# A fused RWKV-6 attention and token mixer: stores moved to the SP queue, and the engines' orders taken from one explicit table of steps

## The chip, the core and the metric

One of the eight cores of a Trainium2 chip runs the whole program. The time is device microseconds from start to end of one execution. The kernel before takes 123.53 us (median of 4 runs beside the new kernel, 122.84 to 123.75). The profile is one traced execution; its span (122.0 us before) is a little shorter than the device time.

Engines in the profile: PE is TensorE's matmuls, PEld its weight loads, DVE is VectorE, ACT is ScalarE, POOL is GpSimd, SP is the engine that here only issues DMAs. A name with q (ACTq, SPq) is that engine's sequencer.

## The reference

Batch 4, 8 heads, 768 tokens, head size 48. A linear attention with a decaying state, then a mixer over tokens:

```python
# attention, per batch and head, t = 0..767
y[t]  = r[t] @ (state + (u * k[t]) ⊗ v[t])
state = w[t][:, None] * state + k[t] ⊗ v[t]
# mixer, x = y as [batch, 768, 384]
W   = (x @ w_q) @ (x @ w_k).T / sqrt(64)      # no softmax, so it is associative
out = relu(W @ x) @ w_out
```

The kernel works in chunks of 128 tokens, two chunks to a unit: 12 units of 256 tokens, 3 units to a batch. With logs of w summed over a chunk by matmuls, r and k are scaled by decays, and the attention of a chunk becomes ordinary masked products, plus a product with the state.

## The kernel before

Each unit n goes through some thirty steps. Those that matter here, with the engine of each (cut; `T` holds the tiles by name):

```python
def load(n, nm, ap):   # SP: 384 KB; three buffers for each of w, k, r, v
    t = ld.tile([C, H, D2], F32, name=nm + "G", tag=nm + "G")
    nc.sync.dma_start(out=t, in_=src.rearrange("h (p j) d -> p h (j d)", j=2))
def log(n):    nc.scalar.activation(pad(T["lw", n]), jhd(T["w", n]), ACT.Ln, ...)    # ACT, reads w
def sums(n):   ...   # PE: cw = prefix sums of the logs
def expk(n), expr(n), decay(n): ...  # ACT: exp(-cw), exp(cw), the chunk's decay
def kdec(n):   nc.gpsimd.tensor_tensor(pad(T["Kd", n]), jhd(T["k", n]), ...)         # POOL, reads k
def rdec(n):   nc.vector.tensor_tensor(pad(Rd)[:, j], jhd(T["r", n])[:, j], ...)     # DVE, reads r
def vcast(n):  nc.scalar.copy(V2, jhd(T["v", n]))                                    # ACT, reads v
def uk1(n), uk2(n): ...  # POOL: k*u, then times r;   red(n): DVE sums it;  vd(n): POOL, times v
def trR(n, j), evT(n): ...   # PE transposes Rd and Kd into PSUM; DVE copies them out (RKT)
def amat(n, js), mask(n, js): ...    # PE scores, DVE mask multiply
def state(n), stadd(n, q), stev(n, q): ...     # PE, PE, DVE: the state after each chunk
def ymat(n), yst(n), yd(n), yev(n): ...        # PE: Y from scores, state, diagonal; copied out as X
def xtr(n), xev(n), qkmat(n), qkev(n): ...     # X transposed, its q and k
# per batch b: tmat, tev, mix, mixev, fin, finev, store
def yst(n):
    for q in range(2):
        if 2 * m + q:
            for hp in range(NP):
                mm(T["Y", n][:, q, ds(hp * D2, D2)], T["RKT", n][:, 0, q, hp],
                   SB[:, ds(hp * D2, D2)], start=False)
```

The order of an engine's instructions is that of a plan: each step has an offset from the start of its unit, the units start some 7.6 us apart, and the plan is sorted by time. All inner units share one list of offsets (`steps`), the first and the last have their own. Tuples of 0 and 1 (`EX`, `ET`, `EQ`, `EM`, `EF`) choose for each PSUM copy between VectorE and ScalarE; `ES` does so for the issuing queue of each half store.

```python
steps = [(-3.67, log, ()), (-1.33, uk1, ()), (-0.45, sums, ()), (-0.42, expk, ()), ...   # cut
start = [0.42, 8.84, 16.14, 23.73, 31.34, 38.86, 46.52, 54.11, 61.53, 69.25, 76.58, 84.42]
```

## Time and profile before

| What | kernel before |
|---|---|
| device time, median | 123.53 us |
| span of the profiled execution | 122.0 us |
| first prefix sum on TensorE | 7.08 us |
| TensorE busy from there to its last matmul | 98.6 us |
| TensorE idle from there to its last matmul | 9.9 us |
| after the last matmul | 6.4 us |

The last four rows add up to the span; they are taken with the end of the last matmul at 115.58 us. (The prediction cuts at 115.2 us and so has 98.2 and 6.8 for the second and the last.) Only idle time of TensorE, its start and the tail can be won, since the matmuls stay.

### The profile page before, as it was taken

The numbers are of one execution on the slowest core, as the hardware profiler recorded it, in microseconds if no ns is written. First come the engines' busy times: TensorE is split into PE (matmuls) and PEld (weight loads), VectorE is DVE, ScalarE is ACT, GpSimd is POOL, SyncE is SP. The second block draws the span as 40 slices with busy tenths as digits, with TensorE's granted clock in tenths as the row PEclk, the third lists the DMA queues.
The fourth block names the chain that finished last, engine by engine and source line by source line (L and its number), as shares of the span: only waits on it lengthen the run. The fifth ranks groups of instructions, "written<-read, shape, count | busy, mean of one in ns | idle before, by whom it ended". The sixth has DMA issues, their size and how long they took to land.

```text
span 122.0 us, 4284 instructions
## 1 busy us (share of the span) xinstructions
PE 100.1 (82%) x1822; PEld 64.6 (53%) x1822; DVE 91.8 (75%) x150; ACT 77.2 (63%) x146; POOL 84.7 (69%) x81
## 2 busy tenths in 40 slices
PE   0193938979898999999999899999999999966800
PEld 0133536557575766757657466576576666532400
DVE  6213596699798978999989998989989777253800
ACT  4236391689779868986685948976478966426000
POOL 8949899995999999599597995967839804000000
PEclk9999996799999999999999999999999999999985
DMA  3999999999999999899839999500552200573092
GB/s 77 322 325 325 323 320 341 292 232 318 236 256 273 288 300 263 230 266 247 245 75 329 348 269 252 149 0 0 134 129 52 82 5 0 129 181 85 24 283 83
DMA packets 54598, 24.66 MB, mean 202 GB/s; under 512 B 51121, under 2 KB 54578, under 8 KB 54578
## 3 DMA queue, kind: packets, MB, share of 16 engines
q1 hardware_dynamic: 52274, 21.24, 64.6%
q10 hardware_dynamic: 2304, 3.15, 9.1%
q8 instruction: 14, 0.23, 0.7%
q14 instruction: 6, 0.05, 0.1%
HBM read 19.66 MB, written 4.72 MB: 200 GB/s over the span
## 4 chain that ended last, share of the span: by engine, by line
PE 68%; ACT 12%; DVE 6%; DMA 3%; POOL 3%; issue 2%; ACTq 1%; SPq 1%; DVEq 0%
PE cw L66 12%; PE Y L66 11%; PE psT L66 10%; PE fps L66 10%; PE Sn L66 5%; PE A L66 5%; PE xt_ps L66 5%; PE qk L66 5%; PE Tps L66 4%; ACT X L130 3%; DMA u<-in_u_dram 3%; DVE AmB L244 3%; ACT XT L130 2%; PE mps L66 2%; POOL uk L250 1%
## 5 line engine op out<-in xcount | busy, mean ns | idle before, releaser
L244 DVE TENSOR_TENSOR AmB<-A,MASK 128x1024 bf16<-128x1024 f32 x24 | 28.8, 1219 | 1.3 <-PE A L66 1.2
L271 POOL TENSOR_TENSOR Vd<-V,diag 128x768 bf16<-128x768 bf16 x12 | 17.7, 1478 | 13.7 <-ACT X L130 3.4
L250 POOL TENSOR_TENSOR uk<-kG,ubc 128x768 f32<-128x768 f32 x12 | 21.8, 1816 | 1.7 <-DVE ubc L486 1.7
L178 ACT ACTIVATE em<-cw,bias 128x384 bf16<-128x384 f32 x24 | 13.0, 580 | 15.6 <-PE cw L66 15.6
L257 POOL TENSOR_TENSOR uk<-uk,rG 128x768 f32<-128x768 f32 x12 | 21.8, 1816 | 0.1
L207 POOL TENSOR_TENSOR KdS<-kG,em 128x768 bf16<-128x768 f32 x12 | 19.7, 1640 | 1.2 <-ACT em L178 1.2
L227 DVE COPY RKT<-psT 128x2048 bf16<-128x2048 bf16 x12 | 14.6, 1217 | 4.0 <-PE psT L66 4.0
L66 PEld LDWEIGHTS <-KdS 64*128 64x128 bf16 (+1 forms) x256 | 10.8, 99 | 9.1 <-POOL KdS L207 3.6
L200 DVE TENSOR_TENSOR RdS<-rG,cw 128x384 bf16<-128x384 f32 x24 | 12.2, 551 | 4.5 <-ACT cw L185 4.5
L66 PE MATMUL fps<-wout_sb,mixT 128*128 128x384 bf16 x72 | 14.6, 328 | 0.1
L302 DVE TENSOR_TENSOR SB<-Sn,pt 128x384 bf16<-128x384 f32 x20 | 11.0, 551 | 4.0 <-PE Sn L66 2.6
L66 PEld LDWEIGHTS <-RKT 48*64 48x64 bf16 (+1 forms) x464 | 10.3, 107 | 7.1 <-issue 4.5
L185 ACT ACTIVATE cw<-cw,bias 128x384 f32<-128x384 f32 x24 | 12.3, 553 | 0.2
L264 DVE TENSOR_REDUCE diag<-uk 128x16 f32<-128x768 f32 x12 | 11.3, 945 | 0.4 <-POOL uk L257 0.4
L155 ACT ACTIVATE logw<-wG 128x768 bf16<-128x768 f32 x12 | 10.2, 851 | 2.1 <-DMA wG<-in_w_dram 2.1
L66 PE MATMUL cw<-logw,BI 128*128 128x384 bf16 x36 | 11.5, 377 | 0.0
L66 PE MATMUL psT<-ID,KdS 128*128 128x128 bf16 x96 | 7.8, 227 | 4.0 <-DVE AmB L244 2.0
L66 PE MATMUL cw<-logw,BS 128*128 128x384 bf16 x36 | 11.0, 363 | 0.0
L66 PE MATMUL A<-RKT 48*64 48x128 bf16 x384 | 10.1, 226 | 0.8 <-ACT X L130 0.8
L130 ACT CAST X<-Y 128x768 bf16<-128x768 f32 x11 | 8.8, 800 | 2.9 <-PE Y L66 2.7
L211 ACT CAST V<-vG 128x768 bf16<-128x768 f32 x12 | 10.0, 841 | 0.0
L130 ACT COPY osb<-fps 128x384 f32<-128x384 f32 x13 | 6.1, 484 | 5.3 <-PE fps L66 2.1
(74 smaller groups left out, 165.1 us busy)
## 6 DMA issues: line engine op xcount, KB each, us to landing
wG<-in_w_dram SPq DMA_DIRECT2D x12, 384.0 KB, 5.5
kG<-in_k_dram SPq DMA_DIRECT2D x12, 384.0 KB, 5.1
rG<-in_r_dram SPq DMA_DIRECT2D x12, 384.0 KB, 4.8
vG<-in_v_dram SPq DMA_DIRECT2D x12, 384.0 KB, 4.9
out_dram<-osb ACTq DMA_DIRECT2D x16, 192.0 KB, 3.0
out_dram<-osb SPq DMA_DIRECT2D x8, 192.0 KB, 3.8
wout_f<-in_moe_w_out_dram SPq DMA_DIRECT2D x1, 576.0 KB, 4.7
wq_f<-in_moe_w_q_dram SPq DMA_DIRECT2D x1, 96.0 KB, 4.1
```

The costliest lines, as they stand in the source:

```text
L66: nc.tensor.matmul(o, l, rr, start=start, stop=stop, skip_group_check=True, is_transpose=trans)
L130: (nc.scalar.copy if e else nc.vector.tensor_copy)(o, i)
L178: nc.scalar.activation(em[:, j], T["cw", n, 1 + j][:, 0:DM], ACT.Exp, bias=bias[2 + j], scale=-1.0)
L185: nc.scalar.activation(cw, cw, ACT.Exp, bias=bias[j], scale=1.0)
L200: nc.vector.tensor_tensor(pad(Rd)[:, j], jhd(T["r", n])[:, j], T["cw", n, j][:, 0:DM].rearrange("p (h d) -> p h d", d=D), ALU.mult)
L207: nc.gpsimd.tensor_tensor(pad(T["Kd", n]), jhd(T["k", n]), hd(T["em", n]), ALU.mult)
L227: nc.vector.tensor_copy(RKT, T["psT", n])
L244: nc.vector.tensor_tensor(T["AmB", n][:, js].rearrange("p q h t -> p h q t"), T["A", n, js], _rep(_rep(MASK[:, js], 1, NP), 1, 2), ALU.mult)
L250: nc.gpsimd.tensor_tensor(uk, T["k", n].rearrange("p h (j d) -> p h j d", j=2), _rep(ubc.rearrange("p (h d) -> p h d", d=D), 2, 2), ALU.mult)
L257: nc.gpsimd.tensor_tensor(uk, uk, T["r", n].rearrange("p h (j d) -> p h j d", j=2), ALU.mult)
L264: nc.vector.tensor_reduce(diag.rearrange("p j h -> p h j"), T["uk", n], axis=AX.X, op=ALU.add)
L271: nc.gpsimd.tensor_tensor(Vd, T["V2", n], _rep(T["diag", n], 3, D), ALU.mult)
```

## The change

The intent: free ScalarE's queue of store issues, balance ScalarE and VectorE anew, and replace the offsets by one explicit order of all 540 steps, laid out by a list schedule, so that a step of any unit can go where there is room for it. The set of steps is the same in both kernels. The diff, cut to its core:

```diff
-    EX = (1, 1, 1, 1, 1, 1, 1, 1, 1, 1, 1, 0)      ...
-    ES = (1, 0, 0, 1, 0, 1, 1, 1, 1, 1, 1, 0, 1, 1, 1, 1, 1, 1, 0, 1, 0, 1, 0, 0)
+    EX = (0, 1, 1, 1, 0, 1, 1, 1, 1, 1, 1, 1)      ...   # EQ and nearly all EF now 1: ScalarE
+    ES = (0, 0, 0, 0, 0, 0, 0, 0, 0, 0, 0, 0, 0, 0, 0, 0, 0, 0, 0, 1, 0, 1, 0, 1)
-    sm = ctx.enter_context(tc.tile_pool(name="sm", bufs=3))
+    sm = ctx.enter_context(tc.tile_pool(name="sm", bufs=5))
     # trR, amat, XT: the two token halves j as an outer dimension of the tiles (cut)
                 for hp in range(NP):
-                    mm(T["Y", n][:, q, ds(hp * D2, D2)], T["RKT", n][:, 0, q, hp],
-                       SB[:, ds(hp * D2, D2)], start=False)
+                    for j in range(2):
+                        mm(T["Y", n][ds(j * HC, HC), q, ds(hp * D2, D2)],
+                           T["RT", n][:, j, hp, ds(q * HC, HC)], SB[:, ds(hp * D2, D2)],
+                           start=False)
-    steps = [(-3.67, log, ()), ...]            # and first, last, bsteps, blast, start, ... (cut)
+    order = (
+        (load, 0, "w"), (load, 0, "k"), (uload,), (load, 0, "r"), (load, 0, "v"),
+        (load, 1, "w"), (load, 1, "k"), (load, 1, "r"), (log, 0), (load, 1, "v"),
+        (load, 2, "w"), (load, 2, "k"), (sums, 0), (load, 2, "r"), (load, 2, "v"),
+        (load, 3, "w"), (expk, 0), (wload,), (decay, 0), (kdec, 0), (ucast,), (expr, 0),
+        ...
+        (stev, 1, 0), (trR, 2, 0), (red, 2), (trR, 2, 1), (log, 4), (stadd, 1, 1), (decay, 3),
+        (vd, 1), (stev, 1, 1), (load, 7, "w"), (log, 5), (evT, 2), (ymat, 1), (vcast, 3),
+        (load, 8, "w"), (yst, 1), (vd, 2), (rdec, 3), (yd, 1), (vcast, 4), (load, 6, "v"),
+        ...
+    )
     with tc.manual_schedule():
-        for _, _, fn in sorted(plan, key=lambda x: x[:2]):
-            fn()
+        for fn, *a in order:
+            fn(*a)
```

(Options for transposes by DMA were added too; they are all off.)

## The prediction

> **What bounds the kernel now.** I read four views in this order: busy shares of the page, busy time in stretches, the early matmuls in the timeline, then the groups by shape and the issue rows of the stores. The page first:
>
> ```profile
> PE 100.1 (82%) x1822; PEld 64.6 (53%) x1822; DVE 91.8 (75%) x150; ACT 77.2 (63%) x146; POOL 84.7 (69%) x81
> PE   0193938979898999999999899999999999966800
> ```
>
> TensorE is busy 82% of 122.0 us, and its row of slices shows where the rest is: at both ends and in holes of the first third. The stretches give the size (columns: from:to, length, then busy us of PE, PEld, DVE, ACT, POOL, then granted clock, DMA share, GB/s):
>
> ```profile
> 8.00:24.00 16.00, 11.58 (x163) 7.75 (x163) 9.28 (x12) 9.46 (x18) 15.39 (x10) 0.89 1.15 323
> 24.00:40.00 16.00, 13.87 (x311) 9.76 (x313) 14.63 (x20) 13.23 (x25) 14.52 (x10) 1.00 1.00 261
> 40.00:60.00 20.00, 19.75 (x384) 13.34 (x383) 18.70 (x28) 15.94 (x30) 17.12 (x11) 1.00 0.99 260
> 60.00:80.00 20.00, 19.18 (x405) 12.50 (x403) 18.72 (x27) 15.57 (x31) 17.78 (x12) 1.00 0.83 233
> 80.00:100.00 20.00, 19.93 (x393) 13.26 (x392) 17.54 (x26) 13.93 (x29) 12.99 (x8) 1.00 0.24 61
> 107.00:115.20 8.20, 5.99 (x54) 3.15 (x54) 4.51 (x10) 2.98 (x7) 0.00 (x0) 1.00 0.37 95
> ```
>
> From 40 to 100 us TensorE idles 60 - 58.86 = 1.1 us: no order can win there. It idles 4.4 us in 8 to 24, 2.1 in 24 to 40, and 2.2 in 107 to 115.2, in all 9.9 us between the first useful matmul at 7.1 us and the last. So 122.0 = 7.1 of start + 98.2 of matmuls + 9.9 of idle + 6.8 after the last matmul (last copy, last stores).
>
> ```profile
> 5.53 1.62 PE L66 MATMUL ups<-u,one 1*128 1x384 f32 x2 [5.53 <-DMA u<-in_u_dram]
> 7.08 0.50 PE L66 MATMUL cw<-logw,BI 128*128 128x384 bf16 x1
> 11.29 1.03 PE L66 MATMUL psT<-ID,KdS 128*128 128x128 bf16 x8 [1.87 <-POOL KdS L207]
> 18.17 0.61 PE L66 MATMUL psT<-ID,KdS 128*128 128x128 bf16 x8 [2.02 <-DVE AmB L244]
> 20.05 1.04 PE L66 MATMUL psT<-ID,RdS 128*128 128x128 bf16 x8
> ```
>
> The start: the broadcast of u stands first on TensorE and holds the prefix sums back until 7.08, though the logarithm they read ended at 4.98. The same eight transposes take 1.03, 0.61 and 1.04 us: until about 16 us and again in 19 to 22.4 us the array runs at half speed. (The granted clock reads 1.00 before its first record, so there the durations decide.)
>
> The rows that price the changed part, each with busy us and mean ns, then the issue row of the stores (shortest, median, longest ns):
>
> ```profile
> L66 PE MATMUL Y<-SB,RKT 128*128 128x96 bf16 x80 | 5.5, 208 | 0.0
> L66 PEld LDWEIGHTS <-RKT 128*128 128x128 bf16 x80 | 3.8, 98 | 0.5
> L66 PEld LDWEIGHTS <-qks 128*64 128x64 bf16 x48 | 2.3, 109 | 1.2 <-DVE qks L130 0.2
> L66 PE MATMUL qk<-XT,wq_sb 128*64 128x128 bf16 x72 | 4.3, 227 | 0.0
> L434 ACTq DMA_DIRECT2D out_dram<-osb x16: 602/626/754, 57.6 to 115.3; - x16
> ```
>
> **What the Trainium skill says.** "TensorE: Matmul & The Clock Gate", Part 1 (the HAM clock gate): the array runs at half clock until one window of about 3.4 us was busy, and falls back after an idle one. The trace agrees: the hole of 2.0 us ending at 18.17 is followed by 3.4 us of slow matmuls. "TensorEngine Tiling (Array Packing)", Restrictions: column tiling turns Fast Weight Load off. The trace agrees weakly: a load of 64 columns takes 109 ns, one of 128 columns 98. "DMA: Bandwidth & Descriptors", Issuing engines are not separate DMA queues: issuing from a second engine saves only the sequencer's time, usually small. Here it is not small: 626 ns of ScalarE's queue each.
>
> **The change part by part.**
> Stores: 16 of 24 issues stand on ScalarE now, 3 afterwards. That frees 13 x 0.626 = 8.1 us of ScalarE's queue and puts as much on SP, which waits mostly.
>
> Copies: ScalarE takes over 6 casts of qks (0.377), 9 copies of osb (0.484), 2 of XT (0.80) and 2 of mixT (0.50), and gives up one of X (0.80): +2.3 + 4.4 + 1.6 + 1.0 - 0.8 = +8.5 us. VectorE loses 6 x 0.42 + 9 x 0.55 + 2 x 0.55 + 2 x 0.55 - 0.96 = 8.7 us. ScalarE's queue comes out even (77.2 + 16 x 0.63 = 87 before, 85.7 + 3 x 0.63 = 88 after), VectorE falls from 92 to 83. Neither is the bound in 40 to 100 us, so this pays only in holes: I count -0.7 us, about a quarter of the 3.2 us idle in 24 to 100, no more, because the new table also has tight spots (the scores of unit 7 are needed 0.65 us of TensorE work after the second score product, while the mask multiply alone takes 1.22).
>
> Layout: transposes, scores, XT and their copies keep count and sizes. Only the product of state and R changes: 4 matmuls of 128x128 weights per chunk become 8 of 128x64, in 20 chunks, so 80 more. Before, 8 of them take 0.45 us from their start to the next group's (52.59 to 53.04): 56 ns each. For 8 of 128x64 with 96 columns the nearest kin is qk from wq_sb, 128x64 and 128 columns alternating between the halves, six in 0.29 us: 48 ns. If the halves overlapped fully, 28 ns (the 64x96 state products); if they follow kin, 48. I take 41: 20 x (8 x 0.041 - 4 x 0.056) = +2.1 us, between 0 and +3.2. With TensorE full this lands on the end.
>
> Start: the prefix sums now come before u, so they start at 5.0 instead of 7.1, and POOL's first K product precedes its u product, about 2.2 us earlier. The u matmul hides in the wait for it. But the early stretch is also bound elsewhere: up to the Y product of unit 1 the table gives VectorE 18.4 us (17.4 before) and ScalarE 20.5 (19.7), by row durations. From an arrival 2.1 us earlier I keep 1.2. A denser start should warm the array one window sooner: matmuls lose some 4.6 us to the half clock now (half of about 6.2 us busy before 15.6 and 3.1 in 19 to 22.4), and I take 0.8 off. Together -2.0 us.
>
> End: before, the X transpose, its copy and qk of the last unit leave TensorE idle 0.46 + 0.65 = 1.1 us; the new table puts output products of batch 2 between them: -1.1 us. The last six copies go from VectorE (2.97 us in one run) to ScalarE, 6 x 0.484 with two issues of 0.63 between: 4.15, so +1.2; the very last pair of stores goes out on two queues, not one after the other: -0.6. Together +0.5 us with rounding against me.
>
> Buffers: five instead of three for the state remove a wait that the trace does not show; 0. Loads on SP keep their lead; 0.
>
> Sum: -0.7 + 2.1 - 2.0 - 1.1 + 0.5 = -1.2 us, 122.1 us against 123.3.
>
> **The rivals.**
> A, the order wins outright: the halves overlap fully (0 instead of +2.1) and the array stays warm from about 9 us (another -1.5). For it: the Tps products, 128x64 too, run twelve of 384 columns in 1.06 us, 88 ns each, where one alone needs some 165. It would make 118.5 to 120.
> B, TensorE's added matmuls win: +3.2, and the early stretch stays VectorE's, so the start keeps 0.5. For it: the kin at 48 ns, and a table that no longer repeats one pattern per unit, units coming in pairs (by rows, ScalarE has 10.0 us of work against TensorE's 5.4 between the Y products of units 0 and 1). Result 124 to 125.
> C, the tail turns into ScalarE's: after the Y product of unit 11 begins, ScalarE has 13.0 us of work against TensorE's 10.9. Against it: most can start at once, and the mix copies are still split 4 to 2. If true, +1 more.
> D, stores and loads on one queue: a store waiting on SP holds a load back. Against it: the last loads stand just after the first stores, 30 us ahead of their use. 0.
>
> **Range and chances.** The terms in doubt are the halves (-2.1 to +1.1 around mine), the early stretch (-2 to +1.5), the middle and tail (-0.5 to +1.5). Together about 2.3 us either way for 8 in 10, a little wider for unmodelled order effects: 119.2 to 125.0. Faster by over 2% means below 120.9, which needs A or luck in two terms: 0.33. Slower means above 125.8: 0.09. Within 2%: 0.58.
>
> **What would show it.** Right: the first prefix sum at 5.0 us; state-times-R row x160 with a stretch of 0.6 to 0.7 us for 16 of them; TensorE busy 1 to 3 us more; VectorE near 83, ScalarE near 86; holes before the last transposes gone; last matmul to end near 7.3 us. Wrong: the 16 products in 0.45 us or less (rival A); holes over 3 us in all between 40 and 100 us, or a first third as long as before (rival B); TensorE waiting on ScalarE's copies after 105 us (C); compute waiting on a load (D). A span below 119 with TensorE no less busy would mean that I underrated the idle that an order can remove.

## The result, and the profile after

The new kernel takes **127.35 us** (126.94 to 128.50, 4 runs) against 123.53 us beside it: ratio 1.0334, 95% interval 1.0254 to 1.0414. A ratio here is the mean time of the one kernel's fast runs over that of the other's in the same rounds, so it is not quite the ratio of the medians. It is slower by 3%, and the predicted range (119.2 to 125.0) missed it. All ratios below are to the kernel before in the same series.

The page of the new kernel, busy shares and TensorE's row of slices:

```profile
PE 99.7 (79%) x1902; PEld 65.3 (52%) x1902; DVE 84.3 (67%) x132; ACT 85.3 (68%) x164; POOL 84.6 (67%) x81
PE   0399688674598877989999997999899999995700
```

VectorE and ScalarE came out as predicted (83 and 86). TensorE has no more work than before, yet there are holes in slices 5 to 16 of 40, some 12.5 to 50 us. In stretches (same columns as in the prediction):

```profile
8.00:24.00 16.00, 12.84 (x216) 8.22 (x216) 12.70 (x17) 11.38 (x22) 15.43 (x10) 1.00 1.12 311
24.00:40.00 16.00, 11.57 (x243) 7.93 (x241) 9.68 (x13) 10.73 (x20) 11.92 (x8) 0.89 1.02 269
40.00:60.00 20.00, 16.98 (x360) 11.32 (x361) 16.73 (x24) 16.10 (x30) 17.38 (x12) 1.00 1.03 274
80.00:100.00 20.00, 19.31 (x407) 13.43 (x407) 18.02 (x22) 13.78 (x30) 16.95 (x11) 1.00 0.27 67
```

Between 24 and 60 us TensorE idles 4.4 + 3.0 = 7.4 us, where it idled 2.1 + 0.25 before. From 24 to 40 us all the other engines are less busy than before too; from 40 to 60 us ScalarE and POOL are about as busy as before. None of them is full, so none is the bound. The granted clock of 0.89 in the second row is one stretch of 3.4 us at half clock (34.1 to 37.5 us); in the 3.4 us before it TensorE idled 1.8 us. The sum by which we compare:

| | before | after | difference |
|---|---|---|---|
| first prefix sum | 7.1 | 5.1 | -2.0 |
| TensorE busy, to its last matmul | 98.6 | 99.7 | +1.1 (the u product, 1.6 us, now lies inside) |
| TensorE idle, to its last matmul | 9.9 | 13.5 | +3.6 |
| after the last matmul | 6.4 | 7.2 | +0.8 |
| span | 122.0 | 125.5 | +3.5 |

The pages also give the chain of work that ended last, followed back from the end, as shares of the span by engine. Before, then after:

```profile
PE 68%; ACT 12%; DVE 6%; DMA 3%; POOL 3%; issue 2%; ACTq 1%; SPq 1%; DVEq 0%
PE 53%; DMA 21%; ACT 9%; issue 4%; POOL 3%; DVE 3%; SPq 2%; ACTq 1%
```

DMA's share of the chain grew from 3% to 21%. The new kernel's chain runs from 23.8 to 43.0 us through three loads and the two ScalarE steps that read them, the V cast and a log (start, length, what; two short pieces lie between):

```profile
23.81 5.86 DMA wG<-in_w_dram
29.70 5.96 DMA vG<-in_v_dram
35.73 0.83 ACT V L211
37.05 5.09 DMA wG<-in_w_dram
42.16 0.84 ACT logw L155
```

Who waits for the loads? The view of waits lists engine and line, what ended the wait, the total us, how many times, and the longest. Of the new kernel:

```profile
ACT logw L155 <- DMA wG<-in_w_dram: 7.3, 6, 2.3
POOL uk L265 <- DMA kG<-in_k_dram: 6.3, 5, 2.6
DVE RdS L200 <- DMA rG<-in_r_dram: 1.3, 2, 1.1
ACT V L211 <- DMA vG<-in_v_dram: 0.4, 1, 0.4
```

Of the kernel before, the one such line of an input (its first load):

```profile
ACT logw L155 <- DMA wG<-in_w_dram: 2.1, 1, 2.1
```

Three engines now wait for inputs, some 15 us in all, of which about 2.2 us is the first load, as before. The traces also tell for each load when it was issued and landed, and when the first instruction that reads it began. For k and w, in us:

| unit | k before: landed, used | k after: landed, used | w before: landed, used | w after: landed, used |
|---|---|---|---|---|
| 3 | 22.6, 26.7 | 26.2, 26.2 | 21.5, 28.1 | 18.8, 18.8 |
| 4 | 28.4, 34.8 | 33.4, 33.5 | 27.1, 34.3 | not told, 26.4 |
| 6 | 34.7, 48.0 | 49.5, 49.7 | 33.5, 48.9 | 34.4, 34.5 |
| 7 | 46.1, 56.1 | 51.4, 51.6 | 45.0, 56.2 | 40.6, 40.7 |
| 9 | 67.6, 71.5 | 62.3, 64.6 | 66.3, 69.7 | 47.1, 47.1 |

Before, an input of these units lies ready 3 to 15 us ahead of its use (unit 5, not shown, had the least: 0.9 us for k, 1.4 for w). After, most are used as they land. The new table asks for the w of unit 9 at 47 us, before the k of units 6 and 7. The queue shows the same from the other side. SP's issues in the new kernel's timeline (start, length, queue):

```profile
17.94 2.25 SPq L150 DMA_DIRECT2D wG<-in_w_dram  x1
20.28 2.32 SPq L150 DMA_DIRECT2D kG<-in_k_dram  x1
22.71 1.01 SPq L150 DMA_DIRECT2D rG<-in_r_dram  x1
23.81 1.10 SPq L150 DMA_DIRECT2D wG<-in_w_dram  x1
25.00 2.17 SPq L150 DMA_DIRECT2D vG<-in_v_dram  x1
27.27 1.17 SPq L150 DMA_DIRECT2D kG<-in_k_dram  x1
```

Each issue keeps SP 1.0 to 2.3 us, one after the other. The page's GB/s row stands at 321 to 335 up to some 22 us, and at 235 to 308 from there to 50 us. At 322 GB/s 384 KB take 1.22 us, at the lower rates 1.3 to 1.7 us. So SP's order is the order of arrival, and about one input arrives per 1.2 to 1.7 us. The k of unit 4, issued at 27.27, stands behind the w of unit 5 and the v of unit 4. POOL pays for it, with the idle time before in brackets:

```profile
26.23 1.81 POOL L265 TENSOR_TENSOR uk<-kG,ubc 128x768 f32<-128x768 f32 x1 [1.26 <-DMA kG<-in_k_dram]
33.51 1.81 POOL L265 TENSOR_TENSOR uk<-kG,ubc 128x768 f32<-128x768 f32 x1 [2.60 <-DMA kG<-in_k_dram]
```

One more comparison, for the product of state and R, in which I expected most of the new cost. The kernel before, then the new one (timelines of TensorE; the group's time is from its start to the next group's):

```profile
52.59 0.51 PE L66 MATMUL Y<-SB,RKT 128*128 128x96 bf16 x8
53.04 0.50 PE L66 MATMUL Y<-Vd,PERM 64*128 64x384 bf16 x4
```

```profile
55.31 0.53 PE L70 MATMUL Y<-SB,RKT 128*64 128x96 bf16 x16
55.77 0.62 PE L70 MATMUL psT<-ID,RdS 128*128 128x128 bf16 x8
```

Sixteen matmuls of 128x64 take 0.46 us, eight of 128x128 took 0.45. This part costs nothing; by these durations the two halves overlap.

### The profile page after: what moved, and what is told of

The parts are those of the page before. It is cut to its first block, busy times and chain, and to the rows that moved or that the text cites. A ratio compares the mean times of both kernels' runs of the same rounds, so it can differ in the third digit from the quotient of the medians.

```text
span 125.5 us, 4453 instructions
## 1 busy us (share of the span) xinstructions
PE 99.7 (79%) x1902; PEld 65.3 (52%) x1902; DVE 84.3 (67%) x132; ACT 85.3 (68%) x164; POOL 84.6 (67%) x81
## 4 chain that ended last, share of the span: by engine, by line
PE 53%; DMA 21%; ACT 9%; issue 4%; POOL 3%; DVE 3%; SPq 2%; ACTq 1%
DMA wG<-in_w_dram 11%; PE Y L70 9%; PE cw L70 9%; PE fps L70 8%; PE psT L70 7%; DMA vG<-in_v_dram 5%; DMA wout_f<-in_moe_w_out_dram 5%; PE Sn L70 4%; PE qk L70 4%; PE A L70 4%; PE Tps L70 3%; PE xt_ps L70 3%; PE mps L70 3%; POOL KdS L207 2%; DVE AmB L259 2%
## 5 line engine op out<-in xcount | busy, mean ns | idle before, releaser
L70 PE MATMUL fps<-wout_sb,mixT 128*128 128x384 bf16 x72 | 13.9, 327 | 0.3 <-DVE mixT L437 0.3
L134 ACT COPY osb<-fps 128x384 f32<-128x384 f32 x22 | 10.0, 482 | 5.5 <-PE fps L70 4.3
L435 ACT ACTIVATE mixT<-mps 128x384 bf16<-128x384 f32 x20 | 8.9, 493 | 2.9 <-PE mps L70 2.8
L134 ACT CAST X<-Y 128x768 bf16<-128x768 f32 x10 | 8.0, 799 | 3.5 <-PE Y L70 3.5
```

The source lines that it names most:

```text
L70: nc.tensor.matmul(o, l, rr, start=start, stop=stop, skip_group_check=True, is_transpose=trans)
L134: (nc.scalar.copy if e else nc.vector.tensor_copy)(o, i)
```

## The theories and the experiments

Theory L: the loads. The table uses inputs earlier and in another order than one queue can bring them, and engines that run strictly in order wait at their head while TensorE runs dry. It has two parts that can be told apart: the order of the loads on SP, and the place in the table of the steps that read them. Theory O, the rival: the table's order of compute steps stalls TensorE by itself (steps too close behind their producers, units bunched in pairs), and the waits on loads only coincide. Side questions: the layout, the stores, the choice of engines, the start, the end.

### 1. Both kernels without loads after unit 2

```diff
 def load(n, nm):
+    if n >= 3:
+        T[nm, n] = T[nm, n - 3]      # compute on the data of units 0 to 2
+        return
```

The result is wrong; all compute steps and their order stay.

> The new kernel with no input loads after unit 2 (units 3 to 11 compute on the data of units 0 to 2; the result is wrong on purpose). Theory L (inputs arrive too late for the new table, TensorE idles behind engines that wait for them): the extra idle of 24 to 60 us goes, 118 to 121.5 us, well below the 123.5 of the kernel before. Theory O (the new table stalls TensorE by its own order of compute steps, loads only coincide): within 1.5 us of the new kernel, 126 to 128 us.

> The kernel before with no input loads after unit 2 (result wrong on purpose). Its trace has no compute wait on a load after the first, so both theories say 122.5 to 123.6 us, unchanged. If it falls by over 1 us, the loads cost the old order something that the waits do not show, such as contention.

Measured: new table 121.67 us (ratio 0.9877, interval 0.9818 to 0.9936), old order 122.41 us (0.9917, 0.9881 to 0.9954). The loads cost the new table 127.35 - 121.67 = 5.7 us and the old order 123.53 - 122.41 = 1.1 us, a little over the 1 us at which I had said that they cost something which the waits don't show. The difference, 4.6 us, less the 0.7 us by which the new table is better without loads, is the 3.8 us of the result. TensorE in the new kernel without loads:

```profile
24.00:40.00 16.00, 14.20 (x345) 10.28 (x345) 13.74 (x18) 14.05 (x25) 16.00 (x11) 1.00 0.02 4
40.00:60.00 20.00, 18.66 (x401) 12.56 (x399) 17.64 (x25) 16.88 (x34) 18.80 (x12) 1.00 0.05 11
```

It idles 1.8 + 1.3 us there instead of 7.4, and the stretch at half clock is gone. Theory O is out as the cause of the loss. What the whole change gains apart from the loads is small: 0.7 us.

### 2. The layout alone

The old order, engines, stores and state buffers in the new kernel's tiles.

> The kernel before (order of steps, engines, stores, three state buffers) with only the new layout: transposes, XT, and the state-times-R product as 160 matmuls of 128x64. In the new trace sixteen of them take 0.46 us, as eight took before, so 123.0 to 124.0 us, no difference. If my predicted cost of 2.1 us were right after all: 125.5.

Measured: 123.55 us, ratio 1.0003 (0.9970 to 1.0037). The layout is free.

### 3. The loads in order of use

```diff
+    # each load goes out in the order in which the table first reads its data,
+    # as soon as the last reader of its buffer has passed (cut)
+    order = by_first_use(order)
```

Compute steps untouched. A second kernel has five buffers per input besides.

> The new kernel with its loads put in the order in which the table first uses them, compute steps untouched. Theory L1 (the order of the loads is at fault: w and v of later units go ahead of k and r of nearer ones): 121 to 124 us. Theory L2 (the table asks for data ahead of the rate at which the queues deliver it, in whatever order): 125 to 127 us, the waits move from k to w. Theory O: 127 us, unchanged.

> The new table with loads in order of use and five buffers per input instead of three, so that almost no load waits for a buffer. Theory L2a (the rate of the queues is the limit): waits on w remain and it stays over 124.5 us. Theory L2b (loads were issued too late because their buffers were still held): 121.5 to 123.5 us.

Measured: the first 124.28, 127.08, 127.29 and 129.07 us, with a granted clock of 0.985 in the fastest and 0.976 in the slowest run. Only the fastest counts as fast, and the three others, the profiled one among them, are slow by the rule for runs (over 1.5% above the fastest). So what the order of loads is worth alone stays undecided. With five buffers 124.93 and 125.93 in the fast runs (ratio 1.0138, 1.0035 to 1.0241), others to 127.9. That is better than the new kernel's 1.0334, but no cure. In the profiled, slow run of the first, the waits on w still come to 6.3 us, those on k to 5.5 and on v to 4.9. So order and buffers together don't cure a table that asks too early, and theory L2 of the expectation, the rate, is left for what remains. By the count of the table, 35 of the 48 loads are read before TensorE has done 32.2 us of its work (steps priced by the rows of the kernel before); in the old order, before 50.5 us. At 1.22 us each, after 4.1 us for the first and with 2.4 us for the weights, the 35th can't land before some 48 us (an estimate from these traces' numbers, and a lower bound, since the rate falls after 22 us). In the traces the 35th load landed at 53.9 us in both kernels: the queue is no slower than before, the table only asks earlier.

### 4. The readers moved later

Three kinds of steps read inputs well ahead of need: the logs (w), the V casts (v) and the first u product (k). They are moved later, to a fixed amount of TensorE work ahead of their own readers, about where the old order had them. TensorE's and VectorE's orders stay as they are.

```diff
+    for what, reader, lead in ((log, sums, 300), (vcast, state, 400), (uk1, uk2, 250)):
+        order = later(order, what, reader, lead)     # lead in 10 ns of TensorE work, units 3 to 11
+    order = by_first_use(order)
```

> The new kernel, correct, with the logs, the V casts and the first u product of units 3 to 11 moved later, to 3.0, 4.0 and 2.5 us of TensorE work ahead of their readers (where the old order had them), and loads in the order of use. TensorE's and VectorE's orders are untouched. Theory L2 (ScalarE and POOL, strict in order, wait at their head for inputs that the table asks for ahead of the rate of the queues): the waits on w and k nearly vanish, 121 to 123.5 us, close to the 121.7 without loads. Rival H (the early logs are what keeps TensorE fed; or SP and the buffers are at fault): 125 us or more.

> The same kernel as late_by_use, whose profile fell into an execution of 445 us on a disturbed chip. Theory L2 as there: fast runs 123 to 125 us (the two of before had 124.2 and 125.6), waits of ScalarE and POOL on w and k under 3 us in all (13.6 in the new kernel).

Measured: of four runs of the first, one took 446.69 us with TensorE busy 97% of the span, a disturbed chip (a run of the kernel before in the same series took 212.4); the fast ones took 125.58 and 124.20 (ratio 1.0094, 0.9979 to 1.0209), the fourth 128.62, a slow one. Repeated, 123.85 us (123.58 to 124.01), ratio 0.9986 (0.9949 to 1.0024). Nearly all of the loss is gone, and of the waits on inputs only the first remains, 2.3 us. Yet it lacks 2.2 us to the run without loads. The stretches show where:

```profile
80.00:100.00 20.00, 16.75 (x361) 11.28 (x360) 15.58 (x20) 12.50 (x25) 15.31 (x10) 1.00 0.17 42
```

TensorE idles 3.2 us in 80 to 100 us; the new kernel idled 0.7 there. In that window VectorE's sum waits 3.1 us for POOL's second u product, two times, and its copy of the transposes, for which TensorE waits, stands behind that sum. So I had moved the u products of the last units too late, with nothing to gain: their k lies ready by then.

### 5. Which of the readers, and does the order of loads matter beside them?

```diff
-    ((log, sums, 300), (vcast, state, 400), (uk1, uk2, 250))
+    late_uk_to_7:     u products only for units 3 to 7
+    late_no_uk:       u products not moved at all
+    late_logs:        logs alone
+    late_by_release:  as late_uk_to_7, but each load where its buffer comes free (as the new table has it)
+    late_by_use_5:    all three, five buffers per input
```

> As late_again, but the u products move later only for units 3 to 7; for 8 to 11, whose k has landed with slack, they stay where the table has them. If the late u products made the 3.3 us of idle TensorE in 80 to 100 us (0.7 in the new kernel): 121 to 122.5 us. If something else: 123.5 to 124.

> Logs and V casts late, u products all where the table has them, loads in order of use. If only ScalarE's early logs were at fault: like late_uk_to_7. If POOL waiting at its head for k is a cause of its own: 1 to 2.5 us slower, with waits of POOL on k of 3 us or more.

> Only the logs late, V casts and u products where the table has them, loads in order of use. If the logs, whose w the queue must bring first, are the whole cause on ScalarE: 122 to 123 us, like late_no_uk. If the early V casts hold ScalarE too: 123.5 to 125.5 us, with waits of V on its load.

> The steps of late_uk_to_7 with each load put where its buffer comes free in the table (as the new table has it) instead of in order of use. If the late steps alone cure it: within 0.7 us of late_uk_to_7. If the order of the loads matters beside them: 1 to 3 us slower.

> Late steps, loads in order of use, and five buffers per input. If rate and order of the loads were all, this comes to the 121.7 of the run without loads, at most 122.5. If it stays at 124 to 125.5, moving the early logs costs something of its own (the casts and logs now stand between ScalarE's copies that TensorE waits for).

| kernel | median us | ratio, 95% interval |
|---|---|---|
| new kernel | 127.35 | 1.0334 (1.0254 to 1.0414) |
| late_by_release | 126.53 | 1.0216 (1.0140 to 1.0291) |
| late_by_use_5 | 126.31 | 1.0153 (1.0088 to 1.0218) |
| late_logs | 124.35 | 1.0066 (1.0014 to 1.0118) |
| late_again | 123.85 | 0.9986 (0.9949 to 1.0024) |
| late_no_uk | 122.21 | 0.9899 (0.9856 to 0.9943) |
| late_uk_to_7 | 122.11 | 0.9868 (0.9832 to 0.9903) |
| new kernel without loads | 121.67 | 0.9877 (0.9818 to 0.9936) |

The medians include slow runs of three kernels (one of 123.57 us in late_uk_to_7, one of 128.21 in late_by_release, one of 127.9 in late_by_use_5); the ratios don't.

Reading it: late_uk_to_7 reaches the kernel without loads within 0.4 us. The u products don't matter (late_no_uk is the same), so POOL's waits for k came from k standing behind w and v in the queue, not from its own place in the table. ScalarE's two early readers, the log and the V cast, matter both: the logs alone leave 2.2 us, and there ScalarE still waits 2.2 us for v (the V casts alone were not run). And the order of loads matters beside them: the same steps with the loads in the new table's manner lose 4.4 us again (4.3 by the ratios). In its trace the chain that ended last goes through a load of r: TensorE's work waits for VectorE's decay of r of unit 4, whose load was issued at 32.8 us and landed at 38.8 (first row below), where late_uk_to_7 had it issued at 26.3 and landed at 31.7. (The profiled run of late_by_release also stayed at half clock until 22.1 us instead of 14.3; I can't split the 4.4 us between the two.) That row of the chain, and the stretches of late_uk_to_7:

```profile
32.83 5.97 DMA rG<-in_r_dram
```

```profile
24.00:40.00 16.00, 13.85 (x341) 9.94 (x334) 13.74 (x18) 13.25 (x24) 14.41 (x10) 1.00 0.91 241
40.00:60.00 20.00, 18.69 (x403) 12.60 (x401) 17.31 (x24) 14.48 (x32) 18.79 (x12) 1.00 0.81 218
80.00:100.00 20.00, 19.31 (x414) 12.72 (x411) 17.10 (x21) 14.26 (x29) 12.14 (x8) 1.00 0.36 96
```

Open stays why five buffers with late steps (126.31) lose to three (123.85). The profiled run has a stretch at half clock from 88.3 to 91.7 us that the other lacks, and loads in flight for longer (median 5.7 us from issue to landing, against 5.0 in late_again), but nothing here proves the cause.

### 6. Stores, and the new engines in the old order

```diff
-    ES = (0, 0, 0, ..., 0, 1, 0, 1, 0, 1)
+    ES = (1, 0, 0, 1, 0, 1, 1, 1, ...)       # after_old_stores: the old choice of queues
```

The second kernel has the old order of steps and everything else of the change.

> The new kernel with the old choice of queue per store (16 on ScalarE's queue, 8 on SP). If stores on SP hold loads back (rival D of the prediction): 125 to 126.5 us. If not: 127 us, or up to 129 since ScalarE's queue pays 13 issues of 0.63 us more.

> The old order of steps, with all else of the change: new engines of copies, stores on SP, new layout, five state buffers. If the order is what loses: 122.5 to 124.5 us, like the kernel before. If the engines or stores lose by themselves (ScalarE's order now holds copies that were placed for VectorE): over 125 us.

Measured: the new kernel with the old stores takes 132.26 us (ratio 1.0689, 1.0600 to 1.0778), worse than either side of my expectation. In the new table, with its copies moved to ScalarE, the 13 issues of 0.63 us are no longer to be had for nothing: stores on SP are worth 4 to 5 us to it (4.9 by the medians, 4.4 by the ratios). Part of that may be the clock: the profiled run with the old stores has 6.8 us at half clock (44.0 to 50.8), and no run splits the two. On balance, then, the stores on SP help. They do hold a load back: in the new kernel the k of unit 10 stands behind stores, is issued at 70.14 us and lands at 74.02, and POOL waits 1.7 us for it. But TensorE is no less busy from 60 to 80 us than before (19.20 against 19.18 us). The old order with the new engines and stores takes 130.51 us (fast runs 128.99 and 129.94; no interval), though the expectation for a bad order was 122.5 to 124.5. So the new engines and stores can't be taken over without the new order. The new order with the old engines of the copies was not run; only the old stores were. I expected either that the engines did no harm or some 2 us; it was 6.

### 7. The start and the end

```diff
 # before_new_start: the kernel before, with
-    at(-99.0, ucast)
+    at(-5.6, ucast)          # u after the first prefix sums; and kdec of unit 0 ahead of its uk1
 # before_start_end: besides, the second half of the last store on ScalarE's queue
 # late_uk_to_7_end: three of the last six output copies on VectorE
-    EF = (..., 1, 1, 1, 1, 1, 1)
+    EF = (..., 0, 1, 0, 1, 1, 0)
```

> The kernel before with the new table's start alone: the u product on TensorE after the first prefix sums, and POOL's first K product before its u product. By my prediction (2.0 us from the start): 121.0 to 122.3 us. Rival: POOL, busy 15.4 of 16 us from 8 to 24 us in both kernels, sets the early stretch, and it begins only 0.4 us earlier: 122.9 to 123.6.

> That start, and the last store's second half on ScalarE's queue so that the last two stores issue side by side: 0.6 us below before_new_start by the issue time of 0.6 us, so 120.4 to 121.7, or 122.3 to 123.0 with the rival. No difference if the landing of the first of the two ends the kernel anyway.

> That, with three of the last six output copies on VectorE instead of all on ScalarE. The last copy then ends some 0.6 us after the last matmul instead of about 2: 1.0 to 1.5 us below late_uk_to_7. If the landing of the last store or its queue sets the end, under 0.5.

Measured: the new start alone gives 123.55 us, ratio 0.9963 (0.9933 to 0.9993): some 0.45 us, not 2. The row of the early stretch shows the rival's reason, in its fifth busy column:

```profile
8.00:24.00 16.00, 12.17 (x154) 7.59 (x152) 9.86 (x13) 7.89 (x14) 15.24 (x10) 1.00 1.15 322
```

POOL is busy 15.2 of 16 us, as it was before (15.4). TensorE starts 2 us earlier, and then waits 3.3 us for VectorE's mask, where it waited 2.0 before. The mask stands behind VectorE's sum, which waits 2.2 us for POOL (the profiled run's timeline, idle time in brackets):

```profile
15.02 0.95 DVE L264 TENSOR_REDUCE diag<-uk 128x16 f32<-128x768 f32 x1 [2.15 <-POOL uk L257]
18.09 1.01 PE L66 MATMUL psT<-ID,KdS 128*128 128x128 bf16 x8 [3.33 <-DVE AmB L244]
```

With the last stores side by side nothing is gained (ratio 0.9993, 0.9959 to 1.0027; its profiled run had a longer stretch at half clock early on, 16.7 to 23.5 us). The copies of the end: 121.74 us, ratio 0.9849 (0.9814 to 0.9883), 0.4 us below late_uk_to_7 by the medians and 0.2 by the ratios. The two intervals overlap, so a gain is not shown. **This version, like late_uk_to_7, beats both kernels**: 1.5% below the kernel before by the ratio, some 4.5% below the new one (4.4% by the medians, which are of different series).

## Why the prediction was wrong, point by point

- **The loads, "Loads on SP keep their lead; 0": this is the step that failed.** It was dismissed with rival D by the last loads alone ("30 us ahead of their use"). The harm was in the loads that the table reads from some 24 to 60 us. Even the last loads kept no such lead: the k of unit 10 landed at 74.0 us and was used at 74.2, that of unit 11 at 80.9 and 82.3. Measured: 5.7 us in the new table, 1.1 in the old order. The evidence was at hand: SP's issues of 1.15 us each and some 320 GB/s over the first fifth of the old page said that the queue was full, and the diff said that logs of units 4 and 5 stand before the Y product of unit 1. I priced each engine's work by sums and never counted at which point of the table each input is first read.
- **Layout, +2.1: wrong in size.** It measured 0 (ratio 1.0003). The kin I chose, the q products at 48 ns, was the wrong one; the 128x64 products of Tps at 88 ns for 384 columns, which I gave to rival A, were nearer: 88 ns for 384 columns is 22 ns for 96, and 0.46 us for 16 makes 29 ns each. The range I allowed, 0 to 3.2, held it.
- **Start, -2.0: the arrival was right, what it is worth was not.** The prefix sums began at 5.11 us as foretold, the first K product at 7.47 (9.59 before), and the array was warm at 13.6 us instead of 15.8. But the start alone, in the old order, gives 0.45 us, because POOL is full. I read POOL's 15.39 of 16 us in the prediction's own fence and counted only VectorE and ScalarE; up to the Y product of unit 1 POOL has 20.6 us of work in the new table by the same row durations, as much as ScalarE's 20.5.
- **Middle, -0.7: not shown by itself.** Without loads the whole change is worth 0.7 us (122.41 to 121.67): middle, layout, start and end together, for which the prediction had -1.2. That these two are close is luck: the layout's +2.1 was 0, so gains foretold as 3.3 us came out as 0.7. I can't give each part its share.
- **End, -1.1: right in kind, somewhat large.** The hole at the last X transpose is gone, but from the Y product of unit 11 to the last matmul TensorE idles 1.4 us where it idled 2.2: 0.8 us less. **+0.5 was somewhat small**: the time after the last matmul grew by 0.8 us. Three copies back on VectorE gave 0.2 to 0.4 us, which is not clear of the spread.
- **Stores, 8.1 us of ScalarE's queue: right**, and worth more than I counted, 4 to 5 us in the new table (with the half clock in it, which is not split off).
- **Rivals.** A was right on the halves and wrong on the time. B came nearest in size (124 to 125, where 127.35 was measured) by the wrong mechanism: neither the halves nor VectorE. Its sign, holes over 3 us between 40 and 100 us, did appear (4.5 us), but the loads made them. C can be at most 0.8 us, the growth of the time after the last matmul. D looked at the right queue and at the wrong loads. Its sign for wrongness, "compute waiting on a load", is what the profile showed.
- **The half clock.** The prediction says that the trace agrees with a fall after an idle window of 3.4 us. It agrees in the length only: before the slow stretch of 19.2 to 22.6 us TensorE was busy for 0.9 of 3.4 us.
- **The sum.** 5.7 - 1.1 = +4.6 us for the loads and -0.7 for all else come to +3.9, against +3.8 measured. These are the same four medians in another order, so the sum is no second proof; it says that the loads are the whole of the loss.

## What to carry to other kernels

Before trusting a new order of steps, list for every input the point at which it is first read, in the time of the bounding engine, and set it against the order and the rate of the queue that brings it; sums of busy time per engine can't show this. As the waits here show, an engine turns one early reader of a late input into a stall for everything behind it, so place readers of inputs late, and issue loads in the order of use. And when a kernel's order is remade, a run without its loads, wrong result and all, splits the loss in one step.

## What the Trainium skill lacked or had wrong

- "DMA: Bandwidth & Descriptors", Issuing engines are not separate DMA queues, says that issuing from more engines saves only sequencer time, usually small. Here that time is 0.63 us per store on ScalarE, and moving 13 of them back to it cost the new kernel 4 to 5 us (ratio 1.0689 against 1.0334; some of it may be a longer stretch at half clock).
- I found no page that gives the time for which an issue on a full queue keeps the sequencer: 1.15 us per 384 KB load here while much is in flight, against 0.37 us for one at 77.6 us with little in flight. The loads of the new kernel that the table above shows arrived in the order of SP's program, so one that waits holds back those behind it.
- "TensorE: Matmul & The Clock Gate", Part 1, lets the clock fall after one idle window of about 3.4 us. The length agrees, but here much less idle time was enough: stretches at half clock of 3.4 us, or twice that, began after 3.4 us in which TensorE idled only 1.8 us (new kernel, before 34.1 us), 1.7 us (new kernel with the old stores, before 44.0 us) and 2.5 us (kernel before, before 19.2 us). A later section of the page, A second HAM failure mode, tells of falls after frequent short idle times and gives no amount. No threshold can be read from these numbers either, and the ends of matmuls are modelled in the trace.
